# Moving half of a weight's column means to a later step, and two jobs from VectorE to ScalarE

## The chip, the cores and the metric

The kernel runs on one core of a Trainium2 chip. A core has a matrix engine (TensorE, "PE" in the profile), three engines for elementwise work (VectorE "DVE", ScalarE "ACT", GpSimd "POOL") and DMA queues. Each engine takes its own list of instructions in order and waits on semaphores for the others. TensorE writes into a small memory of accumulators, PSUM; VectorE and ScalarE read it[...]. The metric is the time of one execution in microseconds on the device, as the median of several runs.

## The reference: what is computed

Two blocks follow each other. The first is attention that keeps, for every query, only the 32 largest scores. The second mixes tokens and channels by a Fourier transform, normalises, and runs a two-layer network.

```python
# attention: q, k, v are (8 batches, 8 heads, 576 tokens, 64), float32
scores = (1 / sqrt(64)) * q @ k.transpose(0, 1, 3, 2)
kth = the 32nd largest of each row
scores = where(scores >= kth, scores, -1e9)
attn = exp(scores - rowmax); attn = attn / (attn.sum(-1) + 1e-9)
x = attn @ v                      # then (8, 576, 512): heads side by side

# Fourier mix and network: w_ch1 (512, 2048), w_ch2 (2048, 512)
mixed = real(fft(fft(x, axis=1), axis=2))
u = x + mixed
un = (u - mean(u)) / sqrt(var(u) + 1e-6)          # over the 512 channels
out = u + maximum(un @ w_ch1, 0) @ w_ch2
```

`(u - mean(u)) @ w1` equals `u @ (w1 - columnmean(w1))`. The kernel uses this: it takes each column's mean off `w1` once ("centring"), and then feeds the network with `u` that was never centred. The scale `1/sqrt(var)` is applied at the very end.

## The kernel before

The program is one long list of steps. A step handles one tile of attention rows: 9 tiles for each pair of heads, 4 pairs for each batch, so 36 steps for each of the 8 batches (`PER_BATCH = 36`). In step `i` VectorE finds the largest 32 scores of a tile (eight passes of `max` and `match_replace`), GpSimd and ScalarE mask and exponentiate an earlier tile, TensorE makes scores for a tile three steps ahead and transposes one that was exponentiated. Two functions place further work into steps: `at(step, where, fn)` appends `fn` to a slot of a step ("pe", "act", "dve", "pool" and others), and a queue of network units fills TensorE's remaining time.

The first 36 steps also load the weights. Each of 32 chunks is split by VectorE (line 162 and 165), converted by ScalarE (177, 179, 183, 184) and joined by GpSimd (192). Centring `w1` comes on top, 512 columns (`c`) at a time:

```python
    def centre(c):
        cols = slice(DM * c, DM * (c + 1))
        cm = ps_s.tile([P, DM], F32, name=f"cm_{c}", tag="sp")
        for dt in range(NDT):
            nc.tensor.matmul(
                cm, lhsT=ones, rhs=w1[:, dt, cols], start=(dt == 0), stop=(dt == NDT - 1)
            )
        mean = means[:, c, :] if c < 3 else sp1[:, 9 * WC:10 * WC]
        def subtract(dt):
            nc.gpsimd.tensor_tensor(
                out=w1[:, dt, cols], in0=w1[:, dt, cols], in1=mean, op=ALU.subtract
            )
        at(now[0] + 1, "convert", lambda: nc.scalar.copy(out=mean, in_=cm))
        for dt in range(NDT):
            at(now[0] + 1 + dt, "pool", lambda dt=dt: subtract(dt))
        return 3.5

    for c in range(DF // DM):
        at(start_of[n1] + 2 + 4 * c, "pe", lambda c=c: centre(c), 3.5)
```

`start_of[n1]` is 17, so the four products run at steps 19, 23, 27 and 31, and GpSimd has one subtraction in each of steps 20 to 35. The product `cm` lies in one of the two score buffers of PSUM (tag "sp") until ScalarE has copied it.

When the four pairs of a batch are done, its attention output is scaled by the softmax denominators and put into `x`, token rows by channels:

```python
        def normalise():                       # in to_tokens(pair, ch)
            nc.vector.tensor_tensor(           # line 479: two tiles of 128 rows
                out=x[:, 2 * ch:2 * ch + 2, cols]..., in0=tp[:, 0:2, :]..., in1=rd[:, 0:4]..., op=ALU.mult)
            if ch == 0:
                nc.vector.tensor_tensor(       # line 486: the tile of 64 tail rows
                    out=x[0:TAIL, 4, cols]..., in0=tp[0:TAIL, 2, :]..., in1=rd[0:TAIL, 4:6]..., op=ALU.mult)
        (late_now if at_once else late_next).append(normalise)
```

It runs twice for each pair of heads: for the even chunk (`ch == 0`, three tiles) and the odd one (two tiles). `rd` holds the inverse denominators, which VectorE makes (lines 457 and 460).

Then the tokens are folded (sums and differences of mirrored halves), so that the Fourier transform over tokens becomes two smaller products, one for the even half (`par == 0`) and one for the odd half:

```python
        def moved():                           # tail rows to the partitions of their mirror
            out, in_ = place(0)[0:TH, 2, :], x[TH:TAIL, 4, :]
            if eng[1] is nc.vector and eng[0] is nc.vector:
                nc.vector.tensor_copy(out=out, in_=in_)      # line 533
            else:
                nc.scalar.copy(out=out, in_=in_)             # line 535
...
        if first:                              # batch 0, T0 = 37
            def folds(b=b):
                for par, space in ((0, "own"), (1, "hT")):
                    for op in fold_steps(fold_ops(b, par, (nc.vector, nc.vector), space)):
                        op()
            at(T0, "dve", folds)
            ft, fc = (T0 + 1, T0 + 1), T0 + 1
```

For batch 0 VectorE does all folds at once in step 37; both token transforms (line 605), the channel transform (661), the row statistics and the first hidden units of the network (747) follow in steps 38 and 39. The last batch, too, folds its even half on VectorE alone. Hidden unit `it` reads columns `128*it` to `128*it + 127` of `w1`.

Of the kernel before, what the change touches and what calls it, by code (L numbers as in the profile page):

```python
# [9 lines left out]
F32 = mybir.dt.float32  # L10
# [8 lines left out]
P = 128  # L19
# [40 lines left out]
def kernel(  # L60
# [9 lines left out]
    nc = tc.nc  # L70
    B, H, S, D = q.shape
    DM = H * D
# [392 lines left out]
    def to_tokens(pair, ch, at_once=True):  # L465

        b, hp = divmod(pair, NPB)
        if b not in x_of:
            x_of[b] = batp.tile([P, 5, DM], F32, name=f"x_{b}", tag="x", bufs=2)
        x = x_of[b]  # L470
        xT, rd = xT_of.pop((pair, ch)), rd_of.pop((pair, ch))
        pool, tag = (ps_o, "o") if at_once else (ps_m, "mm")
        tp = pool.tile([P, 4, P], F32, name=f"tpx_{pair}_{ch}", tag=tag)
        for n, t in enumerate(CHUNKS[ch]):
            nc.tensor.transpose(tp[0:ROWS[t], n, :], xT[:, P * n:P * n + ROWS[t]], ident)  # L475
        cols = slice(P * hp, P * (hp + 1))

        def normalise():
            nc.vector.tensor_tensor(  # L479
                out=x[:, 2 * ch:2 * ch + 2, cols].rearrange("p t (e d) -> p t e d", e=2),  # L480
                in0=tp[:, 0:2, :].rearrange("p t (e d) -> p t e d", e=2),
                in1=rd[:, 0:4].rearrange("p (t e) -> p t e", e=2).to_broadcast([P, 2, 2, D]),
                op=ALU.mult,
            )
            if ch == 0:
                nc.vector.tensor_tensor(
                    out=x[0:TAIL, 4, cols].rearrange("p (e d) -> p e d", e=2),
                    in0=tp[0:TAIL, 2, :].rearrange("p (e d) -> p e d", e=2),
                    in1=rd[0:TAIL, 4:6].to_broadcast([TAIL, 2, D]),
                    op=ALU.mult,  # L490
                )

        (late_now if at_once else late_next).append(normalise)
        return 0.14 * len(CHUNKS[ch])


# [8 lines left out]
    def fold_ops(b, par, eng, space="own", mid=None):  # L505

        x = x_of[b]

        if space == "hT":
            sp = batp.tile([P, NIT * CW[0]], F32, name=f"fsp_{b}", tag="hT")

        def buf(n, name):
            if space == "hT":
                return sp[:, 3 * DM * n:3 * DM * (n + 1)].rearrange("p (s c) -> p s c", s=3)
            pool, tag = (batp, ("fold_s", "fold_d")) if space == "own" else (attp, ("PT0", "PT1"))
            return pool.tile([P, 3, DM], F32, name=f"{name}_{b}_{par}", tag=tag[n % 2], bufs=1)  # L520

        got = folded[b, par] = []

        def place(n):
            while len(got) <= n:
                got.append(buf(len(got), ("sd", "zw", "fg")[len(got)]))
            return got[n]

        def moved():

            out, in_ = place(0)[0:TH, 2, :], x[TH:TAIL, 4, :]
            if eng[1] is nc.vector and eng[0] is nc.vector:
                nc.vector.tensor_copy(out=out, in_=in_)
            else:
                nc.scalar.copy(out=out, in_=in_)

        def first(p):
            sd, op = place(0), ALU.add if par == 0 else ALU.subtract
            if p == 0:
                eng[0].tensor_tensor(out=sd[:, 0:2, :], in0=x[:, 0:2, :], in1=x[:, 2:4, :], op=op)  # L540
            else:
                s_ = sd[0:TH, 2, :]
                eng[1].tensor_tensor(out=s_, in0=x[0:TH, 4, :], in1=s_, op=op)

        def second(p):
            pp, ss = PARTS[p]
            s_, z_ = place(0)[pp, ss], place(1)[pp, ss]
            for cols, op in ((slice(0, Q2), ALU.add), (slice(Q2, DM), ALU.subtract)):
                (mid or eng[p]).tensor_tensor(
                    out=z_[:, :, cols], in0=s_[:, :, 0:Q2], in1=s_[:, :, Q2:DM], op=op  # L550
                )

        def third(n, p):
            pp, ss = PARTS[p]
            z_, f_ = place(1)[pp, ss], place(2)[pp, ss]

            def tt(out, up, down, op):
                eng[p].tensor_tensor(out=f_[:, :, out], in0=z_[:, :, up], in1=z_[:, :, down], op=op)

            if n == 0:  # L560
                eng[p].memset(f_[:, :, Q1:Q1 + 1], 0.0)
                eng[p].tensor_copy(out=f_[:, :, 0:DM:Q2], in_=z_[:, :, 0:DM:Q2])
                up, down = slice(1, Q1), slice(Q2 - 1, Q1, -1)
                tt(up, up, down, ALU.add)
                tt(slice(Q1 + 1, Q2), up, down, ALU.subtract)
            else:
                up, down = slice(Q2 + 1, Q3), slice(DM - 1, Q3, -1)
                tt(up, up, down, ALU.subtract)
                tt(slice(Q3, DM - 1), up, down, ALU.add)
                eng[p].tensor_copy(out=f_[:, :, DM - 1:DM], in_=z_[:, :, Q3:Q3 + 1])  # L570

        return {"moved": moved, "first": first, "second": second, "third": third}

    def fold_steps(f):

        def one():
            f["moved"]()
            f["first"](0)
            f["first"](1)

        def two():
            f["second"](0)
            f["second"](1)

        def three(n):
            f["third"](n, 0)
            f["third"](n, 1)

        return [one, two, lambda: three(0), lambda: three(1)]
# [287 lines left out]
    def at(step, where, fn, cost=0.0):  # L877
        plan.setdefault((step, where), []).append(fn)
        costs[step] = costs.get(step, 0.0) + cost
# [4 lines left out]
    WC = 512  # L884
# [18 lines left out]

    ones = batp.tile([P, P], F32, name="ones", tag="yt")
    nc.vector.memset(ones, 1.0 / DM)
    means = batp.tile([P, 3, DM], F32, name="means", tag="fold_d")

    def centre(c):
        cols = slice(DM * c, DM * (c + 1))
        cm = ps_s.tile([P, DM], F32, name=f"cm_{c}", tag="sp")  # L910
        for dt in range(NDT):
            nc.tensor.matmul(
                cm, lhsT=ones, rhs=w1[:, dt, cols], start=(dt == 0), stop=(dt == NDT - 1)
            )
        mean = means[:, c, :] if c < 3 else sp1[:, 9 * WC:10 * WC]

        def subtract(dt):
            nc.gpsimd.tensor_tensor(
                out=w1[:, dt, cols], in0=w1[:, dt, cols], in1=mean, op=ALU.subtract
            )  # L920

        at(now[0] + 1, "convert", lambda: nc.scalar.copy(out=mean, in_=cm))  # L922
        for dt in range(NDT):
            at(now[0] + 1 + dt, "pool", lambda dt=dt: subtract(dt))
        return 3.5

    for c in range(DF // DM):
        at(start_of[n1] + 2 + 4 * c, "pe", lambda c=c: centre(c), 3.5)

    for b in range(B):  # L930
        end = PER_BATCH * (b + 1) - 1
# [2 lines left out]
        T0 = end + (2 if first else 3 if soon else 4)  # L934
        if first:

            def folds(b=b):
                for par, space in ((0, "own"), (1, "hT")):
                    for op in fold_steps(fold_ops(b, par, (nc.vector, nc.vector), space)):
                        op()  # L940
            at(T0, "dve", folds)
            ft, fc = (T0 + 1, T0 + 1), T0 + 1
        elif soon:

# [233 lines left out]
```

## Time and profile before

| | |
|---|---|
| median time (3 runs) | 2011.47 us (2010.2 to 2012.25) |
| span of the profiled execution | 2010.3 us |
| TensorE busy | 1863.9 us, 93% |
| VectorE busy | 1641.2 us, 82% |
| ScalarE busy | 1220.3 us, 61% |
| GpSimd busy | 831.2 us, 41% |
| column-mean products (line 912) | 32 instructions, 18.3 us |
| subtractions (line 918) | 16 on GpSimd, 1.27 us each |
| normalisation on VectorE (line 479, line 486) | 64 of 424 ns, 32 of 273 ns |
| move of the tail rows on VectorE (line 533) | 3 of 415 ns |

An average over the span says little here, because the stages have different limits: the weights are loaded in roughly the first 260 us, batch 0 passes from attention to the network between 265 and 300 us, attention of later batches runs beside the network of earlier ones until 1800 us, and the last batch's network ends it. A line of the profile begins with the start in us and the duration; a bracket at its end tells how long the engine was idle before and which instruction ended the wait. A busy TensorE can still be waiting within a group, since ends of its pipelined instructions are modelled.

### The profile page before, as it was taken

The numbers are of one execution on the slowest core, as the hardware profiler recorded it, in microseconds if no ns is written. First come the engines' busy times: TensorE is split into PE (matmuls) and PEld (weight loads), VectorE is DVE, ScalarE is ACT, GpSimd is POOL, SyncE is SP. The second block draws the span as 40 slices with busy tenths as digits, with TensorE's granted clock in tenths as the row PEclk, the third lists the DMA queues.
The fourth block names the chain that finished last, engine by engine and source line by source line (L and its number), as shares of the span: only waits on it lengthen the run. The fifth ranks groups of instructions, "written<-read, shape, count | busy, mean of one in ns | idle before, by whom it ended". The sixth has DMA issues, their size and how long they took to land.

```text
span 2010.3 us, 27513 instructions
## 1 busy us (share of the span) xinstructions
PE 1863.9 (93%) x8626; PEld 1126.1 (56%) x8626; DVE 1641.2 (82%) x3405; ACT 1220.3 (61%) x3008; POOL 831.2 (41%) x1114
## 2 busy tenths in 40 slices
PE   5666679999889999999999999999999999998999
PEld 2333356465555656647565656647565656565655
DVE  7999889999999998988889888988899888853100
ACT  6878737677666766656665667656666667541100
POOL 4779822333433365234532374225533364223000
PEclk9678679999999999999999999999999999998999
DMA  4323100010000100001000001010000001000000
GB/s 128 96 82 100 54 7 19 24 26 24 23 19 24 27 24 24 18 18 26 24 24 13 26 19 29 18 32 18 19 24 24 23 15 30 0 14 1 11 14 11
DMA packets 133584, 57.81 MB, mean 29 GB/s; under 512 B 124352, under 2 KB 124480, under 8 KB 133440
## 3 DMA queue, kind: packets, MB, share of 16 engines
q1 hardware_dynamic: 132208, 55.73, 10.3%
q8 instruction: 69, 1.13, 0.2%
q14 instruction: 75, 0.61, 0.1%
q10 hardware_dynamic: 1232, 0.33, 0.1%
HBM read 46.57 MB, written 9.44 MB: 28 GB/s over the span
## 4 chain that ended last, share of the span: by engine, by line
PE 69%; DVE 12%; POOL 6%; ACT 6%; issue 6%; DMA 0%; SPq 0%; POOLq 0%; DVEq 0%
PE cp L771 20%; PE hp L747 20%; PE o L430 7%; PE sp L328 5%; PE tpP L393 5%; DVE m L349 5%; DVE wk L351 4%; PE yp L605 3%; POOL wk L366 3%; PE cp L807 2%; PE mp L661 2%; PE sp_t L298 1%; POOL w L192 1%; ACT wk L365 1%; ACT wk L372 1%
## 5 line engine op out<-in xcount | busy, mean ns | idle before, releaser
L366 POOL TENSOR_TENSOR wk<-S,wk 128x576 f32<-128x576 f32 x288 | 406.9, 1413 | 864.9 <-ACT wk L365 833.6
L349 DVE MAX8 m<-wk 128x8 f32<-128x576 f32 x864 | 623.1, 749 | 5.4
L747 PE MATMUL hp<-unT,w 128*128 128x256 f32 (+1 forms) x2048 | 538.3, 409 | 3.7 <-POOL t L709 2.2
L771 PE MATMUL cp<-w,hT 128*128 128x512 f32 x1024 | 479.3, 600 | 0.0
L747 PEld LDWEIGHTS hp<-unT,w 128*128 128x128 f32 x2048 | 372.7, 190 | 128.2 <-issue 32.2
L351 DVE MATCH_REPLACE8 wk<-m,wk 128x576 f32<-128x576 f32 x576 | 427.6, 742 | 0.0
L771 PEld LDWEIGHTS cp<-w,hT 128*128 128x128 f32 x1024 | 179.6, 190 | 183.6 <-issue 182.8
L372 ACT ACTIVATE wk<-wk,nt 128x576 f32<-128x576 f32 x288 | 225.0, 781 | 79.2 <-POOL wk L366 77.8
L365 ACT ACTIVATE wk<-S,nt 128x576 f32<-128x576 f32 x288 | 226.3, 786 | 50.0 <-POOL nt L358 47.8
L393 PE MATMUL tpP<-ident,wk 128*128 128x128 f32 x1152 | 186.8, 287 | 73.0 <-ACT wk L372 38.0
L396 ACT COPY PT<-tpP 128x512 f32<-128x512 f32 (+1 forms) x320 | 170.7, 544 | 117.4 <-PE tpP L393 114.9
L349 DVE MAX8 m<-S 128x8 f32<-128x576 f32 x288 | 214.1, 743 | 32.8 <-ACT S L302 32.5
L393 PEld LDWEIGHTS tpP<-ident,wk 128*128 128x128 f32 x1152 | 140.3, 146 | 174.2 <-ACT wk L372 56.7
L751 ACT ACTIVATE hT<-hp 128x320 f32<-128x320 f32 (+1 forms) x256 | 104.6, 409 | 192.2 <-PE hp L747 190.0
L351 DVE MATCH_REPLACE8 wk<-m,S 128x576 f32<-128x576 f32 x288 | 213.7, 742 | 0.0
L430 PE MATMUL o<-PT,v 128*64 128x256 f32 (+3 forms) x1440 | 195.9, 414 | 4.6 <-ACT PT L396 4.1
L331 ACT COPY S<-sp 128x512 f32<-128x512 f32 (+1 forms) x264 | 141.9, 588 | 73.3 <-PE sp L328 73.0
L328 PE MATMUL sp<-kT,qT 64*128 64x512 f32 (+1 forms) x528 | 168.1, 690 | 2.3 <-ACT means L922 1.9
L430 PEld LDWEIGHTS o<-PT,v 128*64 128x64 f32 x1440 | 111.5, 153 | 78.1 <-issue 14.6
L192 POOL TENSOR_TENSOR w<-w,space 128x512 f32<-128x512 f32 x96 | 123.6, 1287 | 8.6 <-ACT space L183 5.7
L785 DVE SCALAR_TENSOR_TENSOR x<-cp,gi,x 128x512 f32<-128x512 f32 x11 | 8.2, 746 | 128.3 <-PE cp L771 128.3
L479 DVE TENSOR_TENSOR x<-tpx,rd 128x256 f32<-128x256 f32 x64 | 27.1, 424 | 73.7 <-PE tpx L475 71.0
(125 smaller groups left out, 1899.0 us busy)
## 6 DMA issues: line engine op xcount, KB each, us to landing
space<-in_moe_w_ch_dram SPq DMA_DIRECT2D x32, 512.0 KB, 3.5
nat<-in_q_dram SPq DMA_DIRECT2D x128, 64.0 KB, 2.0
v<-in_v_dram SPq DMA_DIRECT2D x128, 64.0 KB, 2.1
out_dram<-x SPq DMA_DIRECT2D x32, 256.0 KB, 2.1
nat<-in_k_dram SPq DMA_DIRECT2D x124, 64.0 KB, 2.1
nat<-in_q_dram SPq DMA_DIRECT2D x128, 8.0 KB, 1.7
v<-in_v_dram SPq DMA_DIRECT2D x128, 8.0 KB, 1.7
nat<-in_k_dram SPq DMA_DIRECT2D x124, 8.0 KB, 1.7
```

What stands on the lines that cost most here:

```text
L192: nc.gpsimd.tensor_tensor(out=dst, in0=dst, in1=(low, high, ex)[part], op=ALU.mult if part else ALU.add,)
L328: nc.tensor.matmul(sp[r], lhsT=qT[hd, q_cols], rhs=kT[hd, :], start=True, stop=True)
L349: ops.append(lambda src=src, m8=m8: nc.vector.max(out=m8, in_=src))
L351: ops.append(lambda src=src, m8=m8: nc.vector.match_replace(w, m8, src, NEG))
L365: nc.scalar.activation(out=w, in_=Ssb[i], func=AF.Relu, scale=-FAR, bias=Nt[i][:, 1:2])
L366: nc.gpsimd.tensor_tensor(out=w, in0=Ssb.pop(i), in1=w, op=ALU.subtract)
L372: nc.scalar.activation(out=w, in_=w, func=AF.Exp, bias=Nt.pop(i)[:, 0:1], accum_out=den_t[pair % 3][:, c:c + 1],)
L393: nc.tensor.transpose(tp[:, c, :], p_sb[:, k0 + P * c:k0 + P * (c + 1)], ident)
L396: nc.scalar.copy(out=pt[:, NF * he:NF * (he + 1), col:col + w], in_=tp[:, :, o:o + w])
L430: nc.tensor.matmul(o[D * e:D * (e + 1), c0:c1], lhsT=vv[:, c, e, :], rhs=pt[:, 2 * NF if c == NF else NF * e + c, c0:c1], start=(c == 0), ...
L747: nc.tensor.matmul(hp[:, 0:w], lhsT=w1[:, dt, P * it:P * (it + 1)], rhs=unT[:, dt, 0:w], start=(dt == 0), stop=(dt == NDT - 1),)
L771: nc.tensor.matmul(cp, lhsT=hT[:, it, P * n:P * (n + 1)], rhs=w2[:, it, :], start=(it == 0), stop=(it == NIT - 1),)
```

## The change

It has four parts. The second half of the column means (`c` = 2 and 3) leaves the load stage: their products come at steps 36 and 37, their subtractions all at once in steps 39 and 40, before the network reaches these columns. The first half stays in the load stage, with the products at steps 19 and 27. This relieves GpSimd and TensorE while weights are being joined. The means of the second half get a tile of their own in the space of `x`. Next, the move of tail rows for folds done wholly by VectorE goes to ScalarE, ahead of the folds. Last, the normalisation of batch 1's output, all but its last piece, goes from VectorE to ScalarE, one step later, as single copies of 64 columns with a scale for each row. The aim is to take work off the engines that are full in each stage.

```diff
-        (late_now if at_once else late_next).append(normalise)
+        def normalise_on_act():
+            for n, t in enumerate(CHUNKS[ch]):
+                r = slice(0, ROWS[t])
+                for e in range(2):
+                    hd = slice(D * e, D * (e + 1))
+                    nc.scalar.mul(
+                        out=x[r, t, cols][:, hd], in_=tp[r, n, hd],
+                        mul=rd[r, 2 * n + e:2 * n + e + 1],
+                    )
+
+        if b == 1 and (hp, ch) != (NPB - 1, 1):
+            at(now[0] + 1, "act", normalise_on_act)
+        else:
+            (late_now if at_once else late_next).append(normalise)
@@ moved
-            if eng[1] is nc.vector and eng[0] is nc.vector:
-                nc.vector.tensor_copy(out=out, in_=in_)
-            else:
-                nc.scalar.copy(out=out, in_=in_)
+            nc.scalar.copy(out=out, in_=in_)
@@ fold_steps(f) becomes fold_steps(f, moved=True); with moved=False it leaves the move out
@@ centre
-    means = batp.tile([P, 3, DM], F32, name="means", tag="fold_d")
+    mean_of = {0: batp.tile([P, 2, DM], F32, name="means", tag="fold_d")}
-    def centre(c):
+    def centre(c, early):
...
-        mean = means[:, c, :] if c < 3 else sp1[:, 9 * WC:10 * WC]
+        if c == DF // DM // 2:
+            mean_of[1] = batp.tile([P, 2, DM], F32, name="means_1", tag="x", bufs=2)
+        mean = mean_of[2 * c // (DF // DM)][:, c % 2, :]
...
         for dt in range(NDT):
-            at(now[0] + 1 + dt, "pool", lambda dt=dt: subtract(dt))
+            s0 = now[0] + 1 + dt if early else now[0] + 3
+            at(s0, "pool", lambda dt=dt: subtract(dt))
...
     for c in range(DF // DM):
-        at(start_of[n1] + 2 + 4 * c, "pe", lambda c=c: centre(c), 3.5)
+        early = c < DF // DM // 2
+        at(
+            start_of[n1] + 2 + 8 * c if early else PER_BATCH - 2 + c, "pe",
+            lambda c=c, early=early: centre(c, early), 3.5,
+        )
@@ folds of batch 0
-            def folds(b=b):
+            def folds(b=b, T0=T0):
                 for par, space in ((0, "own"), (1, "hT")):
-                    for op in fold_steps(fold_ops(b, par, (nc.vector, nc.vector), space)):
-                        op()
-            at(T0, "dve", folds)
+                    f = fold_ops(b, par, (nc.vector,) * 2, space)
+                    at(T0, "act", f["moved"])
+                    for op in fold_steps(f, False):
+                        at(T0, "dve", op)
+            at(T0, "begin", folds)
```

More of the change, by code (lines that the diff above doesn't have):

```diff
@@ L572, in fold_ops, with fold_steps @@
         return {"moved": moved, "first": first, "second": second, "third": third}
-    def fold_steps(f):
+    def fold_steps(f, moved=True):
         def one():
-            f["moved"]()
+            if moved:
+                f["moved"]()
             f["first"](0)
```

## The prediction

> **What bounds the kernel now.** I first cut the span into stages by the busy time of each engine (columns: stretch in us; busy time of PE, weight loads, VectorE, ScalarE, GpSimd, with instruction counts; granted TensorE clock; DMA share; GB/s).
>
> ```profile
> 155.00:215.00 60.00, 37.85 (x184) 21.50 (x183) 56.79 (x116) 49.60 (x111) 58.38 (x55) 0.84 0.32 94
> 215.00:265.00 50.00, 31.38 (x134) 18.81 (x133) 38.97 (x80) 30.20 (x72) 35.57 (x34) 0.64 0.15 39
> 265.00:300.00 35.00, 28.94 (x135) 20.73 (x134) 31.30 (x77) 12.29 (x34) 5.61 (x12) 0.80 0.00 1
> 300.00:500.00 200.00, 198.87 (x946) 117.37 (x945) 193.84 (x398) 139.53 (x348) 66.26 (x88) 1.00 0.10 23
> 500.00:565.00 65.00, 57.01 (x299) 37.90 (x298) 64.09 (x139) 39.55 (x102) 30.53 (x46) 0.95 0.08 20
> 565.00:1800.00 1235.00, 1218.69 (x5819) 732.13 (x5818) 1084.65 (x2260) 804.32 (x2014) 509.99 (x738) 1.00 0.09 21
> ```
>
> From 565 to 1800 TensorE is idle for 16 us of 1235, so it sets the pace there, with the same work before and after the change. What is won earlier is therefore kept, and what matters is the stretch before 565. In 155 to 215 GpSimd is full (58.4 of 60). In 215 to 265 nobody is full, VectorE least expected of all: it lacks 11 us. From 300 to 565 VectorE has no gap except one of 2.8 us (258 of 265 us), and TensorE is full too until 500, then idles 8 us.
>
> Next, VectorE's own order of time in 226 to 266, with idle time and its releaser in brackets:
>
> ```profile
> 226.53 0.69 DVE L162 TENSOR_SCALAR wm<-space 128x512 int32<-128x512 int32 x1
> 231.16 0.69 DVE L165 TENSOR_SCALAR we<-space 128x512 int32<-128x512 int32 x1 [3.94 <-ACT w L177]
> ...
> 233.22 0.76 DVE L349 MAX8 m<-S 128x8 f32<-128x576 f32 x1 [0.71 <-ACT S L302]
> ...
> 244.58 0.30 DVE L457 TENSOR_SCALAR rd<-den 128x6 f32<-128x6 f32 x1 [1.88 <-ACT den L449]
> ...
> 248.53 0.76 DVE L349 MAX8 m<-S 128x8 f32<-128x576 f32 x1 [2.04 <-ACT S L302]
> ...
> 259.47 0.76 DVE L349 MAX8 m<-S 128x8 f32<-128x576 f32 x1 [0.67 <-ACT S L302]
> ...
> 265.15 0.42 DVE L479 TENSOR_TENSOR x<-tpx,rd 128x256 f32<-128x256 f32 x1 [1.00 <-PE tpx L475]
> ```
>
> And the chain of waits through the same time, for what stands behind the first gap:
>
> ```profile
> 222.99 5.75 PE cm L912 x8
> 228.74 0.45 PE tpP L393 x4
> 229.21 0.58 ACT PT L396
> 229.80 0.17 ACT PT L405
> 229.97 0.67 ACT wk L365
> 230.64 0.49 ACT w L177
> ```
>
> The reader is to see one cause. The last column-mean product (line 912) keeps TensorE for 5.75 us at the low clock; the transposes behind it come late, ScalarE waits for them with its copy (396), and the weight conversion (177) that VectorE's second split (165) needs stands behind that copy. Later on the same chain two subtractions of the last chunk of columns stand between joins and masks, at 250.0 and 253.7.
>
> [...] the granted clock is 0.50 in 220 to 225, 0.55 in 250 to 255 and 1.00 from 290 on, and the same eight instructions of line 912 took 3.67 us at 140.7 and 5.75 us at 223.0. [...] Here a 128x143 copy (638) takes 302 ns and the same with a scale operand (639) 414 ns, so 0.11 us.
>
> **The change, part by part.** (T is when the last normalisation before batch 0's folds starts, now 265.15.)
>
> 1. Steps 23 to 31. The second product goes from step 23 to 27, and its subtractions from 24–27 to 28–31. GpSimd's masks come every 6.62 us in steps with a subtraction (187.02 to 193.64: mask 1.4, three joins 3.9, subtraction 1.27), VectorE's splits every 6.14 us where it doesn't wait (187.59 to 193.73). So steps 24–27 become VectorE's. I add what VectorE idles: the interval 166.27 to 174.27 is 8.00 against 6.14, 1.86 too long, by the product at 165.96 (5.07 us); I take 1.5 of it. In 193.73 to 200.47 it loses 0.6, in 213.72 to 220.39 0.5, both with GpSimd behind; with the backlog cleared in 24–27 I take both. Sum: -2.6 us.
>
> 2. Steps 31 to 37. No product in step 31, no subtractions in 32–35. The gaps 3.94 and 0.71 go: -4.65. The later gaps 1.88, 2.04 and 0.67 (4.6 together) are ScalarE and TensorE catching up, with GpSimd's 4 x 1.27 in between; I take 3.3 of them. With part 1 this is -10.5 at T, 254.6. Were VectorE never idle, T would be about 252.
>
> Can TensorE follow, with the third product (c=2) in step 36? It stands after the q transposes (ending 256.6 now) and before the last tile's transposes (260.04 now, released by ScalarE; 3.4 us idle). At 3.7 to 5.8 us it takes the gap and 0.3 to 2.3 us more. At the new pace VectorE ends step 37 some 2 us after the tokens of the last tile could be there, so this about fits, and 0 is charged: the 1.3 us of gaps left in this part stand for it.
>
> 3. Step 37 and 38. The fourth product (c=3) comes after batch 1's 64-row scores (now 265.05) and before the tail scores. It waits until ScalarE has copied the first of these out of the two score buffers (about T+1.4), takes 5 to 5.8 us (T+7), and the next scores need its buffer back: mean copy to about T+8.9, two score products to T+10.5. So the token transform of the even half starts near T+10.5, now T+6.4 (271.54). It takes 6 us, and the odd half's 7.05 then start at T+16.5 instead of T+14.2 (279.33). Cost: +2.3 us.
>
> 4. The move of the tail rows. Two copies of 0.41 us (533) leave VectorE; a 32x512 copy on ScalarE takes 0.62 (535), where ScalarE has 23 of 35 us free. VectorE's odd fold is ready 0.9 us sooner, but by part 3 TensorE is late for it: 0. In the last batch one such copy (0.43 us at 1819.58) lies on the chain to a TensorE gap of 8.71 us that ends with the fold; there it counts: -0.4 us.
>
> 5. Subtractions at steps 39 and 40, 4 x 1.27 = 5.1 us each. The first four fall into GpSimd's free time between 303.9 and 311.0. The second four start about 312.6 and end at 317.7, and mask 40 (now 315.29) moves by 2.4 us, its exponential (now 317.88) by 1.2. TensorE's next transposes of that tile come at 323.5, so nearly nothing is lost: +0.3. The hidden layer's ninth block, the first that reads the late columns, runs at 328.
>
> 6. Batch 1's normalisation. Seven of eight go: on VectorE an even one costs 0.54 us from start to start (331.81 to 332.35), an odd one 0.34. 4 x 0.54 + 3 x 0.34 = 3.2 us, in a stretch where VectorE has no gaps until 563. ScalarE takes 6 or 4 instructions of 128x64 instead: a copy of that form 215 ns, with the scale operand some 0.3 us, so 1.8 and 1.2 us, 10.8 in all, against 60 us that it has free in 300 to 500. But TensorE is only 1.1 us short of full there, and gets idle time only after 500. I take three quarters: -2.4.
>
> Sum: -10.5 + 2.3 - 0.4 + 0.3 - 2.4 = -10.7 us. From 2011.5 this gives **2000.8 us**.
>
> **The rivals.**
> - *The products only change their place.* The two moved products run at low clock where the path is as narrow (the last tile's transposes, the folds' transforms), and what step 31 gives is taken back in 36 to 38. For it: the clock is 0.5 to 0.55 in half of the 5 us slices there, and 7.4 us each (3.7 at half clock) would cost about 2 us more at T and 2 at the transforms. Against it: TensorE idles 3.4 us before the tile's transposes and 4 of the 15 us from 265 to 280. It would give about -5: 2006.
> - *TensorE bounds batch 1.* It is full until 500, so the 3.2 us of VectorE only open gaps in VectorE, and the extra ScalarE work delays buffers for TensorE. For it: 198.9 of 200 busy. Against it: VectorE has no gap in all that time, and after 500 TensorE waits for it. Then part 6 is 0 or +1: 2003.
> - *The first stage gives more.* VectorE becomes gapless from 174 to T, and TensorE, now without a pause before the folds' transforms, gets its full clock there: the odd half at 280 to 286 runs at 0.50 and could fall from 7 to 5 us. Then -15 to -17: 1995.
>
> **Range and chances.** The largest term is part 2, 5 to 10 us by how many of the later gaps close; part 3 may be 0 to 4, part 6 0 to 3.2. Together the range that holds 8 in 10 is 1994 to 2006.5. A change of 2% would be 40 us; the gaps and subtractions concerned are not worth more than 17 us, and no added wait is near 40. Chances: faster by over 2% 0.01, within 2% 0.98, slower 0.01.
>
> **What would show it.** Part 1 and 2: no product between steps 27 and 36, the masks of steps 24–27 about 6.15 us apart, VectorE's five blocks of steps 33–37 each near 5.1 us, T near 254.6. Part 3: the odd half's transform starting 15 to 17 us after T; if it is 18 or more, the first rival holds. Part 5: mask 40 late, TensorE without a gap from hidden block to hidden block. Part 6: VectorE still gapless from step 41 to the statistics of batch 1, and these some 2.4 us closer to the start of batch 0's hidden layer; if VectorE shows gaps on ScalarE or TensorE instead, the second rival holds. I am wrong if the time is above 2006.5, most likely by the two moved products, or if a difference arises after 600.

## The result, and the profile after

| | before | after |
|---|---|---|
| median, in runs taken together | 2010.84 us (2009.45 to 2012.25, 6 runs) | 2004.12 us (2003.44 to 2004.36, 6 runs) |
| ratio | | 0.9966 [0.9953, 0.9979] |
| span of the profiled execution | 2010.3 us | 2002.2 us |

The change takes off 6.7 us where 10.7 had been predicted. (The same program measured again, further down, was only 0.8 us below before; where the difference lies is said there as far as it is known.) I first give the profile after, then a division of the span into stages that all experiments use.

The busy time of each engine by stretch, after (columns: stretch in us; length; busy time of PE, weight loads, VectorE, ScalarE, GpSimd, with instruction counts; granted TensorE clock; DMA share; GB/s):

```profile
155.00:215.00 60.00, 36.42 (x177) 21.73 (x177) 59.26 (x119) 49.96 (x112) 54.32 (x52) 0.76 0.32 94
215.00:265.00 50.00, 33.03 (x155) 18.54 (x153) 45.16 (x98) 34.24 (x81) 31.28 (x31) 0.75 0.15 40
265.00:300.00 35.00, 30.91 (x157) 23.80 (x159) 28.61 (x69) 11.10 (x30) 13.44 (x24) 0.90 0.00 0
300.00:500.00 200.00, 198.11 (x945) 115.78 (x942) 193.73 (x393) 144.67 (x383) 73.80 (x89) 1.00 0.10 25
500.00:565.00 65.00, 50.73 (x271) 33.45 (x269) 64.02 (x137) 41.11 (x107) 30.88 (x50) 0.94 0.10 23
565.00:1800.00 1235.00, 1224.57 (x5852) 737.75 (x5851) 1077.86 (x2247) 804.48 (x2011) 506.13 (x725) 1.00 0.09 21
```

In 155 to 215 the full engine has changed from GpSimd (58.4, now 54.3 of 60) to VectorE (56.8, now 59.3). In 215 to 265 VectorE lacks 5 us instead of 11. From 300 to 500 GpSimd and ScalarE have 7.5 and 5.1 us more to do, the late subtractions and the normalisation; the rest is nearly the same there.

VectorE in order of time through the end of the load stage, after (start, duration; a bracket is idle time and its releaser):

```profile
226.02 0.68 DVE L162 TENSOR_SCALAR wm<-space 128x512 int32<-128x512 int32 x1
226.61 0.68 DVE L165 TENSOR_SCALAR we<-space 128x512 int32<-128x512 int32 x1
...
237.98 0.27 DVE L457 TENSOR_SCALAR rd<-den 128x6 f32<-128x6 f32 x1 [0.64 <-ACT den L449]
...
241.93 0.76 DVE L349 MAX8 m<-S 128x8 f32<-128x576 f32 x1 [2.07 <-ACT S L302]
...
256.99 0.42 DVE L479 TENSOR_TENSOR x<-tpx,rd 128x256 f32<-128x256 f32 x1
```

The gap of 3.94 us between the two splits (162, 165) is gone. Of the three later gaps the one of 2.04 stays, the one of 1.88 shrinks to 0.64, the one of 0.67 is gone. T, the last line, is 256.99 instead of 265.15.

GpSimd's masks (366) on either side of step 31, first before, then after:

```profile
220.15 1.41 POOL L366 TENSOR_TENSOR wk<-S,wk 128x576 f32<-128x576 f32 x1
230.72 1.41 POOL L366 TENSOR_TENSOR wk<-S,wk 128x576 f32<-128x576 f32 x1 [3.94 <-ACT wk L365]
```

```profile
218.67 1.42 POOL L366 TENSOR_TENSOR wk<-S,wk 128x576 f32<-128x576 f32 x1
225.29 1.40 POOL L366 TENSOR_TENSOR wk<-S,wk 128x576 f32<-128x576 f32 x1
```

The interval falls from 10.57 to 6.62 us, the pace that GpSimd keeps in the steps around it. This one step is more than half of the whole gain.

And TensorE at batch 0's token transforms before:

```profile
271.54 3.89 PE L605 MATMUL yp<-fs,fg 128*128 128x145 f32 x16 [0.84 <-DVE fg L558]
...
279.33 7.05 PE L605 MATMUL yp<-fs,fsp 128*128 128x145 f32 x30 [1.81 <-DVE fsp L558]
```

and, from the late products on, after:

```profile
249.17 3.60 PE L924 MATMUL cm<-w,ones 128*128 128x512 f32 x8
...
257.91 3.70 PE L924 MATMUL cm<-w,ones 128*128 128x512 f32 x8 [0.89 <-ACT S L320]
...
264.90 2.25 PE L617 MATMUL yp<-fs,fg 128*128 128x145 f32 x16
...
271.15 7.15 PE L617 MATMUL yp<-fs,fsp 128*128 128x145 f32 x30 [1.91 <-DVE fsp L569]
```

Both late products (924) run at full speed (granted clock 1.00 from 248 to 270), 3.6 and 3.7 us, and the 16 instructions that open the even half's transform take 2.25 us, against 3.89 before (0.51 in 268 to 272, 0.63 in 272 to 276). But ahead of the odd half TensorE still pauses for VectorE's fold, 1.91 us where it was 1.81, its clock falls in this pause from 1.00 to 0.50 (at 270.4) as it did before (at 278.4), and the odd half takes 7.15 us, before 7.05.

**The stages.** The first column-mean product (c = 0, step 19; "product 0" below) is the same in every kernel here, and it starts anywhere from 137.97 to 141.09 us without any system. So I count from it. T is as in the prediction; "hidden" is batch 0's first hidden unit, "last" the first token transform of the last batch. All times in us, one profiled execution each.

| kernel | product 0 to T | T to hidden | hidden to last | last to end |
|---|---|---|---|---|
| before | 124.4 | 34.6 | 1531.5 | 179.1 |
| normalisation alone | 124.1 | 34.6 | 1531.3 | 179.2 |
| late subtractions alone | 124.1 | 37.8 | 1531.5 | 182.5 |
| batch 1's normalisation left out | 124.1 | 37.8 | 1531.5 | 182.5 |
| **after** | 117.2 | 34.7 | 1531.5 | 179.1 |
| after, repeated | 117.2 | 34.7 | 1531.4 | 182.5 |
| means alone | 117.2 | 34.7 | 1531.4 | 179.1 |
| without normalisation | 117.3 | 37.9 | 1531.6 | 179.1 |
| the same, repeated | 117.3 | 37.9 | 1531.6 | 179.2 |
| late half left out | 117.6 | 32.6 | 1533.1 | 179.1 |
| pause filled | 117.2 | 32.1 | 1534.2 | 179.0 |
| move a step early, without normalisation | 117.8 | 31.1 | 1531.4 | 179.1 |
| move a step early, with normalisation | 117.8 | 31.1 | 1533.0 | 181.6 |
| move two steps early, without normalisation | 117.1 | 31.1 | 1534.1 | 178.9 |

Two things are read from it. What the change does to the work is in the first column, 124.2 (the mean of the four above) to 117.2: -7.0 us. And most of what else differs fits the clock: columns two and four take values about 3.4 us apart.

### The profile page after: what moved, and what is told of

Read it like the earlier page. It is cut to its first block, busy times and chain, and to the rows that moved or that the text cites. A ratio compares the mean times of both kernels' runs of the same rounds, so it can differ in the third digit from the quotient of the medians.

```text
span 2002.2 us, 27534 instructions
## 1 busy us (share of the span) xinstructions
PE 1856.8 (93%) x8626; PEld 1122.8 (56%) x8626; DVE 1639.2 (82%) x3391; ACT 1230.1 (61%) x3047; POOL 835.0 (42%) x1114
## 3 DMA queue, kind: packets, MB, share of 16 engines
q1 hardware_dynamic: 132208, 55.73, 10.5%
## 4 chain that ended last, share of the span: by engine, by line
PE 70%; DVE 12%; issue 6%; ACT 6%; POOL 6%; DMA 0%; POOLq 0%; DVEq 0%; ACTq 0%
PE cp L783 20%; PE hp L759 19%; PE o L430 7%; PE sp L328 5%; PE tpP L393 5%; DVE m L349 5%; DVE wk L351 4%; PE yp L617 3%; POOL wk L366 2%; PE cp L819 2%; PE mp L673 2%; PE sp_t L298 2%; ACT wk L365 1%; ACT wk L372 1%; POOL w L192 1%
## 5 line engine op out<-in xcount | busy, mean ns | idle before, releaser
L298 PEld LDWEIGHTS sp_t<-kt,qT 128*128 128x128 f32 (+1 forms) x322 | 51.7, 188 | 62.6 <-issue 23.8
```

## The experiments

### The three parts, one at a time

*Means alone*: the change without the normalisation on ScalarE and without the move on ScalarE, so only the column means differ from the kernel before.

> Only the later half of the column means, as in the change; the tail rows are moved by VectorE and batch 1 is normalised by VectorE, as before. My theory (the whole gain is the load stage's, and the two late products cost nothing): the network of batch 0 starts about 8 us earlier than the 299.7 us of before, the time is 7 to 9 us below before, at least as good as the whole change. Rival (the normalisation carries a part of the gain, as I predicted with 2.4 us): 4 to 5 us below before.

*Normalisation alone*: the kernel before, with batch 1's normalisation on ScalarE.

> The kernel before with only batch 1's normalisation given to ScalarE. My theory (TensorE sets the pace of batch 1 until about 490 us, VectorE only gets gaps): VectorE is about 2.5 us ahead at 470 us and then waits for the token transposes and GpSimd's fold; the time is 0 to 1 us above before. Rival (VectorE sets the pace): 2 to 3 us below before.

*Without normalisation*: the change, with the one line of before in place of the added branch.

> The changed kernel with batch 1's normalisation back on VectorE. My theory: 0.5 to 1 us below the changed kernel, so 7 to 8 us below before. Rival (normalisation helps by 2.4 us): 4 to 5 us below before.

```diff
 means alone / without normalisation (both): against the change
-        if b == 1 and (hp, ch) != (NPB - 1, 1):
-            at(now[0] + 1, "act", normalise_on_act)
-        else:
-            (late_now if at_once else late_next).append(normalise)
+        (late_now if at_once else late_next).append(normalise)
```

| | median (range, runs) | ratio to before |
|---|---|---|
| means alone | 2004.11 us (2002.47 to 2006.55, 4) | 0.9956 [0.9941, 0.9971] |
| normalisation alone | 2010.62 us (2008.85 to 2016.6, 20) | 0.9996 [0.9989, 1.0003] |
| without normalisation | 2007.89 us (2006.57 to 2008.76, 9) | 0.9978 [0.9969, 0.9988] |

The means alone have the whole gain, the normalisation alone has none. The third run was a miss: 4 us slower than the means alone, although only the move of the tail rows separates them. Its trace is like that of the change up to 277 us and then differs in the clock. Here are stretches around it, of the change and then of the kernel without normalisation (columns as in the stage view above; the granted clock is third from the end):

```profile
266.00:270.00 4.00, 3.25 (x24) 2.30 (x22) 4.00 (x8) 1.48 (x7) 3.66 (x1) 1.00 0.00 0
270.50:277.00 6.50, 5.85 (x23) 4.37 (x23) 6.50 (x21) 0.00 (x0) 0.45 (x2) 0.50 0.00 0
277.50:284.00 6.50, 6.49 (x32) 4.72 (x31) 3.76 (x8) 2.04 (x7) 0.00 (x0) 1.00 0.01 3
```

```profile
266.00:270.00 4.00, 3.29 (x24) 2.35 (x22) 4.00 (x8) 1.48 (x6) 3.61 (x1) 1.00 0.00 0
270.50:277.00 6.50, 5.80 (x23) 4.33 (x23) 6.50 (x21) 0.00 (x0) 0.49 (x2) 0.50 0.00 0
277.50:284.00 6.50, 6.50 (x19) 5.30 (x18) 1.55 (x3) 2.15 (x7) 0.00 (x0) 0.50 0.01 3
284.50:290.00 5.50, 5.50 (x25) 3.95 (x25) 4.06 (x9) 0.00 (x0) 0.00 (x0) 1.00 0.00 0
```

In the first, half clock lasts until about 277.2, in the second until about 284.1, with TensorE busy for all of the extra time: 19 instructions where the other did 32. In slices of half a microsecond the two episodes (stretches of half clock) are 6.83 and 13.65 us long. In the change 8 instructions of line 617 take 2.27 us at a granted clock of 0.50 (at 1823.12) and 16 of the same form 2.25 us at 1.00 (at 264.90), so half of the time at half clock is lost. By an estimate from these numbers the longer episode costs 3.4 us more (half of 13.65 less 6.83), which is about the step between the values in the stage table (34.6, 37.9; 179.1, 182.5).

### Is it the products or the subtractions?

*Late subtractions alone*: the kernel before, all four products where they were, and only the subtractions of c = 2 and 3 moved to steps 39 and 40. It frees GpSimd of what the change frees it of, but not TensorE.

```diff
+        if c == DF // DM // 2:
+            mean_of[1] = batp.tile([P, 2, DM], F32, name="means_1", tag="x", bufs=2)
...
-            at(now[0] + 1 + dt, "pool", lambda dt=dt: subtract(dt))
+            s0 = now[0] + 1 + dt if early else PER_BATCH + 1 + c
+            at(s0, "pool", lambda dt=dt: subtract(dt))
```

> The kernel before with only the subtractions of the later half in steps 39 and 40; its two products stay in the load stage (steps 23 and 31). If the product of step 31 is the main cost there (my reading of the trace before: gaps of VectorE of 3.94 us and the ones after it), the last normalisation before the folds starts only 2 to 4 us earlier than the 265.15 us of before. If GpSimd's subtractions are the cost (rival), it starts 6 to 8 us earlier, as in the changed kernel (257.0 us).

Measured: 2010.62 us (2008.09 to 2017.39, 20 runs), ratio 1.0001 [0.9994, 1.0007]. Product 0 to T is 124.05 against 124.1 to 124.4: nothing, less than either theory had. The work that GpSimd loses is not what held the stage: with it gone, GpSimd only waits longer ahead of the mask of step 31, 5.78 us instead of 3.94.

```profile
228.67 1.40 POOL L366 TENSOR_TENSOR wk<-S,wk 128x576 f32<-128x576 f32 x1 [5.78 <-ACT wk L365]
```

What held the stage are the products in TensorE's order, step 31's above all. Whether the subtractions would cost anything once the product is gone is not shown, since no run moves the products alone. In the change GpSimd idles 0.89 to 3.68 us ahead of each of the four masks that follow the one at 225.29, and a subtraction takes 1.27.

*Late half left out*: the change without normalisation, and without the products and subtractions of c = 2 and 3 altogether (these columns stay uncentred).

```diff
-    for c in range(DF // DM):
+    for c in range(DF // DM // 2):
```

> The changed kernel without batch 1's normalisation on ScalarE, and with the later half of the column means left out altogether (products, copies, subtractions), so that half of w1 stays uncentred: the price of the late half. If the late products cost nothing because they fill pauses of TensorE and keep its clock at full speed, the normalisation before the folds starts at most 1 us earlier than 257.0 us, the even half's transform runs slower again (3 to 4 us for its first 16 instructions in place of 2.25), and from that normalisation to the first hidden unit it takes 34 us or more. If they cost what I predicted (2.3 us), it takes 32 to 33 us, and the time is 2 to 3 us below the changed kernel.

Measured: 2004.36 us (2002.29 to 2005.24, 8 runs), ratio 0.9966 [0.9955, 0.9976]. T does not come earlier (117.6 from product 0), so the product at step 36 costs nothing. The even half's first 16 instructions take 4.24 us instead of 2.25, about as long as in before (3.89), where the granted clock was 0.51 to 0.63 there; in the change it is 1.00, so by these times the late products keep TensorE's clock up. T to hidden was a miss, 32.6 where 34 or more was expected, and lies in the 32 to 33 us of the other side. But the late products do not delay the odd half: without them it starts later, at T+14.7 instead of T+14.2. It is shorter, 4.57 us instead of 7.15, because the slow even half ends later and leaves a pause of only 0.31 us ahead of it.

### The pause before the odd half

*Move a step early*: without normalisation, and ScalarE moves batch 0's tail rows at step 36, so that VectorE need not wait 1.43 us for this copy in the middle of its folds.

```diff
-                    at(T0, "act", f["moved"])
+                    at(T0 - 1, "act", f["moved"])
-            at(T0, "begin", folds)
+            at(T0 - 1, "begin", folds)
```

> As the previous one, and ScalarE moves batch 0's tail rows at step 36 instead of 37, ahead of batch 1's score copies. If VectorE's wait of 1.43 us for that move (seen in the changed kernel's trace at 260.1 us) is on the path, the folds end 1.4 us earlier; TensorE's pause before the odd half's transform falls from 1.9 to about 0.5 us, and if the low clock of that transform (7.15 us) comes from the pause it falls to about 4 us: together 3 to 5 us below the previous run. Rival (the pause does not matter for the clock, or TensorE is late anyway): 0 to 1.4 us below the previous run.

*Pause filled*: the change, with four products of 128x256 that nobody reads, put into TensorE's order between the two halves.

```diff
+                def fill():
+                    junk = ps_s.tile([P, DM], F32, name="junk", tag="sp")
+                    for _ in range(4):
+                        nc.tensor.matmul(
+                            junk[:, 0:DM // 2], lhsT=ident, rhs=fd[:, 0, :], start=True, stop=True
+                        )
...
+                at(ft[par], "pe1", fill)
```

> The changed kernel with four products of 128x256 that nobody reads, put into TensorE's pause of 1.9 us before the odd half's transform. If the pause costs the clock (granted 1.00 before it and 0.50 for 6 us after it), the odd half falls from 7.15 to 4 to 5 us and the time by 2 to 3 us, though TensorE does more. If the clock falls for another reason, the odd half stays at 7 to 8 us and the time rises by 0 to 0.5 us.

TensorE at the two transforms, first with the move a step early, then with the pause filled:

```profile
266.34 2.25 PE L603 MATMUL yp<-fs,fg 128*128 128x145 f32 x16
...
270.97 4.56 PE L603 MATMUL yp<-fs,fsp 128*128 128x145 f32 x30 [0.28 <-DVE fsp L555]
```

```profile
265.35 2.25 PE L617 MATMUL yp<-fs,fg 128*128 128x145 f32 x16
...
269.63 1.99 PE L1001 MATMUL junk<-fd,ident 128*128 128x256 f32 x8
271.61 4.56 PE L617 MATMUL yp<-fs,fsp 128*128 128x145 f32 x30
```

In both the odd half takes 4.56 us, against 7.15 in the change (all 30 instructions) and 8.08 without normalisation. So the pause is what drops the clock here: with junk in it, and nothing else changed, the episode is absent (granted clock 1.00 in all of 256 to 292), and T to hidden falls from 34.7 to 32.1. The times: the early move 2001.03 us (1999.62 to 2002.37, 4 runs), ratio 0.9939 [0.9922, 0.9955]; the filled pause 2004.51 us (2002.29 to 2004.71, 5 runs), ratio 0.9967 [0.9954, 0.998]. The first is 6.9 us below the run without normalisation, more than the 3 to 5 expected, because that run's half clock had lasted 13.7 us and not 6.8 as in the change; by the estimate above that costs 6.8 us, as much as T to hidden differs (37.9 and 31.1). For the second I had expected 2 to 3 us less than the change. What it won at 271 us it lost again by batch 3's first token transform (945 us): hidden to last is 2.7 us longer, about half of it lost before 727 us and half behind, where its trace has a new episode of 3.4 us near 790 (granted clock 0.79 in 788 to 796).

*Move two steps early*: as above, with `T0 - 2`.

> The change without the normalisation on ScalarE, and with batch 0's tail rows moved two steps early (at step 35). My theory: the move at step 36 delayed ScalarE's other copies and with them T by 0.8 us; at step 35 ScalarE has more room, so T comes back to about 257.0, TensorE has no pause of more than 1 us before the odd half's transform, the clock stays at full speed there (odd half 4.5 us rather than 7 to 8), and the time is 0 to 1.5 us below the 2001.0 of the move at step 36. Rival (any delay of ScalarE there costs the same): T stays near 257.8 and the time at 2001 or above.

Measured: 2004.02 us (2002.6 to 2005.84, 4 runs), ratio 0.9963 [0.9948, 0.9977]. Its mechanism came out (117.1 to T instead of 117.8, a pause of 0.93 us, no episode, odd half 4.56 us), its time did not: this profile too has an episode near 790 (0.90 in 784 to 788, 0.68 in 788 to 792), after a pause of 1.96 us, and hidden to last is 2.7 us longer, again about half of it ahead of that episode. The kernel with the move one step early has the same pause of 1.96 us there, and its clock stays at 1.00.

### The normalisation, and the change once more

*Normalisation left out*: the kernel before, with seven of batch 1's eight normalisations replaced by GpSimd writing zeros (batch 1's output is not computed). It shows what part 6 could bring at most.

```diff
+        def zeros():
+            nc.gpsimd.memset(x[:, 2 * ch:2 * ch + 2, cols], 0.0)
+            if ch == 0:
+                nc.gpsimd.memset(x[0:TAIL, 4, cols], 0.0)
...
-        (late_now if at_once else late_next).append(normalise)
+        if b == 1 and (hp, ch) != (NPB - 1, 1):
+            at(now[0], "pool", zeros)
+        else:
+            (late_now if at_once else late_next).append(normalise)
```

> The kernel before with seven of batch 1's eight normalisations left out; GpSimd writes zeros in their place, so ScalarE has no more work than before and the output of batch 1 is not the reference's. If TensorE sets the pace of batch 1 (my theory), the stretch from the first hidden unit of batch 0 to the end of batch 1's statistics stays at 263.0 us within 0.5. If VectorE sets it and ScalarE's added work ate the gain (rival), it is 2 to 3 us shorter.

Measured: 2010.94 us (2008.71 to 2017.43, 20 runs), ratio 1.0 [0.9993, 1.0007]; from the first hidden unit to the end of batch 1's statistics 263.29 us, before 263.02. Even with the work gone from both engines nothing is won. VectorE in the change (first), and with the means alone, where VectorE still normalises, shows why:

```profile
482.94 0.42 DVE L479 TENSOR_TENSOR x<-tpx,rd 128x256 f32<-128x256 f32 x1 [1.35 <-PE tpx L475]
...
491.92 3.16 DVE L560 TENSOR_TENSOR zw<-sd 128x512 f32<-128x512 f32 x4 [2.25 <-POOL sd L551]
```

```profile
485.80 0.42 DVE L479 TENSOR_TENSOR x<-tpx,rd 128x256 f32<-128x256 f32 x1
...
491.70 3.17 DVE L549 TENSOR_TENSOR zw<-sd 128x512 f32<-128x512 f32 x4
```

In the change VectorE does the last normalisation 2.9 us earlier, but only after waiting for TensorE's transposes (475), and then waits for GpSimd's fold (551). The fold behind both waits starts at 491.92 and 491.70, 352.1 and 351.7 us after product 0: the lead is all given back.

Three more runs were measured together with the move two steps early, on another chip than the experiments before it.

*The change again*, unaltered:

> The change as it is, on one chip with the next runs. My theory: how long the half clock lasts after the pause of 1.9 us before the odd half's transform is not settled by the program; so this can come out at 2004 with a half clock of 6 us, or at 2007 to 2008 with one of 14 us. Rival (the program settles it): 2004 and 6 us again, to a microsecond.

*Without normalisation, again*, unaltered:

> The change without the normalisation on ScalarE, for a second time. My theory: same code as the change up to that pause, so the 3.5 us between the two came from the length of the half clock and not from the normalisation; from batch 0's first hidden unit to the end of batch 1's statistics both take 263.3 to 263.8 us, and the two times overlap when measured side by side or differ by just what the half clock differs by. Rival (the normalisation on ScalarE is worth 3 us): this one is 3 us slower with a half clock of the same length.

*The change with the move a step early* (the early move above, with the normalisation on ScalarE):

> The whole change, normalisation on ScalarE included, with the move at step 36. With no pause before the odd half the clock has no part in it, so beside the run without the normalisation (2001.0) this tells part 6 alone. My theory (TensorE sets the pace in batch 1): 2000.5 to 2002. The prediction's part 6, or the rival that the normalisation is worth 3 us: 1998 to 1999.

| | median (range, runs) | ratio to before |
|---|---|---|
| the change again | 2010.55 us (2005.2 to 2011.94, 20) | 0.9992 [0.9985, 0.9999] |
| without normalisation, again | 2007.07 us (2002.3 to 2008.83, 13) | 0.9978 [0.997, 0.9987] |
| the change, move a step early | 2005.21 us (2003.68 to 2006.61, 6) | 0.9966 [0.9954, 0.9977] |

The change itself, 2004.12 us in its first six runs, is 2010.55 here, 0.8 us below before instead of 6.7; three of its 20 executions took 2005.2 to 2005.7 us, the others 2009.2 to 2011.9. Neither side of what I had written covers that. The profiled execution is one of the three: its load stage has the full gain (117.2), the half clock at 268.5 lasts 6.8 us again, and the 3.4 us that it has lost lie in the last batch. Granted clock there, third from the end, the change first, then its repeat:

```profile
1817.00:1824.00 7.00, 0.88 (x4) 0.91 (x5) 6.96 (x10) 0.00 (x0) 6.94 (x11) 0.72 0.00 0
1824.00:1831.00 7.00, 6.12 (x26) 4.33 (x26) 3.78 (x9) 0.04 (x1) 4.16 (x8) 0.55 0.00 0
1831.00:1838.00 7.00, 7.00 (x20) 3.27 (x19) 0.00 (x0) 1.70 (x6) 0.00 (x0) 1.00 0.00 0
```

```profile
1817.00:1824.00 7.00, 2.27 (x8) 1.95 (x8) 6.96 (x12) 0.00 (x0) 6.94 (x13) 0.50 0.00 0
1824.00:1831.00 7.00, 6.70 (x23) 4.82 (x24) 1.80 (x6) 1.50 (x6) 2.18 (x5) 0.50 0.00 0
1831.00:1838.00 7.00, 7.00 (x12) 2.83 (x11) 0.00 (x0) 0.33 (x2) 0.00 (x0) 0.70 0.00 0
```

At full load (7.00 of 7.00) the repeat does 12 instructions where the other does 20. Where the 17 longer executions lose another 5 us was not profiled; more such episodes would do it, but that is not shown.

On the normalisation these runs agree with the stage table. From the first hidden unit to the end of batch 1's statistics it takes 263.7 us with the normalisation on ScalarE and 263.4 without, as expected. Side by side, the kernel without it is now 3.5 us *faster* than with it, where in the first runs it had been 3.8 us slower. The two programs are the same both times, so the sign of this difference is not the code's; that the clock makes all of it is not shown, since most executions were not profiled. The early move with the normalisation is 2005.21, not the 2000.5 to 2002 of my theory, because 1.6 us more lie between hidden and last and 2.5 in the last batch. In the last batch half clock lasts 17 us, and 20 instructions there (line 783, at 1832.22) take 10.30 us; without the normalisation they take 8.85, as in the change, where half clock lasts 10 us. Most of the 1.6 us appears near 582, where VectorE waits 2.18 us for TensorE's transposes instead of 0.74; why is open. Its first two columns equal those of the early move without it, to 0.1 us.

## Why the prediction was right, and where it was wrong

The direction, the stage and the cause held in the first measurement: the time fell by less than 2%, inside the range, all of it before T, and through the removed product of step 31. In the second the gain before T was there again in the execution that was profiled, but the median of 2010.55 us lies above 2006.5, from where the prediction had called itself wrong, and only a part of that is traced to half clock. By its own steps:

1. **Part 1 (steps 23 to 31): -2.6 predicted, between -0.2 and +0.5 measured.** This step failed. From product 0 to VectorE's split at the end of this stretch (162 at 226.02, before at 226.53) it takes 86.20 us after, and 85.79, 86.40 and 86.38 in the three kernels with before's early products and subtractions. I had added up VectorE's gaps in the one trace of before. But in that trace VectorE stood 2.9 us further ahead at product 0 than in the other two (its split at 0.97 us ahead of the product, theirs 1.9 behind it), and its gaps only used up that lead. Nor did the longest of these gaps come from the product. The 1.86 us between 166.27 and 174.27 were laid to the product of step 23, but the change with the move a step early, which has no product there and VectorE with before's lead, shows the same gap (first before, then this kernel):

```profile
174.27 0.69 DVE L162 TENSOR_SCALAR wm<-space 128x512 int32<-128x512 int32 x1 [1.07 <-ACT w L177]
```

```profile
174.73 0.69 DVE L162 TENSOR_SCALAR wm<-space 128x512 int32<-128x512 int32 x1 [1.18 <-ACT w L177]
```

   The interval ahead of it is 8.16 us there, before 8.00, and 6.14 in the kernel with the normalisation alone, which has the product and no lead. With the same lead as before, this kernel and the repeat without normalisation reach the split after 86.25 and 86.24 us, 0.5 later than before. Without a lead, VectorE is full at once when GpSimd is relieved, as the 59.3 of 60 show.

2. **Part 2 (steps 31 to 37): -7.9 predicted, -6.8 measured** (from that split to T 37.8 us in the two such kernels beside before, 31.0 after; 38.6 in before, whose split comes 0.6 us sooner). The 4.65 us of the two first gaps went as predicted. Of the 3.3 us from the later gaps somewhat more than half came (1.88, 2.04 and 0.67 became 0.64, 2.07 and none); the gap of 2.07 at 241.93 stays. With part 1 the term of -10.5 should have been -7.0. That the third product would fit in step 36 at no cost held; of a share of the subtractions no run shows anything.

3. **Part 3 (products at steps 36 and 37): +2.3 predicted, 0 measured.** The fourth product came as described, and moved the even half from T+6.4 to T+7.9, not to T+10.5. I charged 5 to 5.8 us for it, as two of the early products took at low clock (5.07 and 5.75), and 6 for the even half. The clock was at 1.00 from 250 to 270, where before had 0.50 to 0.91 in the slices from 256 to 272, because the products themselves fill TensorE's pauses (with them left out, pairs of score products at 259 and 262 take 1.63 and 2.07 us, in the change 1.12): 3.7 us, and 2.25 for the first 16 instructions. The odd half began at T+14.16, before at T+14.18, and in both VectorE's fold released it, so TensorE had another 1.91 us to spare. I had the clock in the third rival only, and did not carry it into the sum.

4. **Part 4 (the move): 0 and -0.4 predicted, 0 measured.** With the means alone, where VectorE moves the rows, T to hidden is the same 34.7 us: in the change VectorE, spared the two copies of 0.41 us, waits 1.43 us for ScalarE's first copy. In the last batch the wait for the fold fell from 8.71 to 8.48 us, and hidden to last shows no difference.

5. **Part 5 (subtractions at steps 39 and 40): +0.3 predicted, 0 within 0.2 measured.** GpSimd and then TensorE in the change:

```profile
304.46 4.98 POOL L933 TENSOR_TENSOR w<-w,means 128x512 f32<-128x512 f32 x4
309.39 1.42 POOL L366 TENSOR_TENSOR wk<-S,wk 128x576 f32<-128x576 f32 x1
```

```profile
315.81 0.65 PE L393 MATMUL tpP<-ident,wk 128*128 128x128 f32 x4 [0.23 <-ACT wk L372]
```

   Mask 40 follows straight upon the four subtractions (4.98 us), and all that TensorE sees of it is 0.23 us.

6. **Part 6 (normalisation): -2.4 predicted, 0 measured.** The second rival was right: VectorE "without a gap" was only keeping step. That it is TensorE that sets the pace of batch 1 is read from its 198.9 busy us of 200 and from VectorE's wait for its transposes. From the first hidden unit to the end of batch 1's statistics the change takes 263.8 us, the means alone 263.4: nothing is won there either. The cost on ScalarE was right for one 128x64 piece, 331 ns where I had 0.3 us, but six in a row overlap and take 1.31 us (at 327.95), not 1.8. Against the 215 ns of a plain copy of this form (302) the scale operand adds 116 ns.

The first rival (products only change their place, 2006) falls: at their new place they cost nothing. The third was right on the clock up to 270 us and wrong at the odd half, where the pause of before, which this rival had thought gone, stayed and dropped it again (to 0.50); with the move a step early its 7 to 5 us is seen (7.15 to 4.56). The sum of what was measured is -7.0 + 0 + 0 + 0 + 0 = -7.0, against -6.7 in the times. That the total came no further off is in part luck: parts 1, 2 and 6 promised 5.9 us too much, part 3 charged 2.3 too much.

The fastest kernel here is the one with the tail rows moved a step early and without the normalisation on ScalarE, 2001.03 us; with that normalisation the same move gave 2005.21, no less than the change's first 2004.12. T to hidden is 31.1 us in all three kernels with an early move, 3.6 less than in the change, and their executions (four to six of each) spread over 2.8 to 3.2 us. With the late products and the pause left in, executions spread over 0.9 to 6.7 us and medians of the same program differ by up to 6.4. What decides between 6.8 and 13.7 us of half clock stays open. The kernel without normalisation had 13.7 both times and the change 6.8 both times, though both do the same work up to there; so do before and the kernel with batch 1's normalisation left out, and in these the odd half took 7.05 and 8.08 us, T to hidden 34.6 and 37.8. So the work ahead of the pause does not decide it alone.

## What to carry to other kernels

A gap on an engine is worth its length only if nothing else sets the pace: before adding gaps up, find out whether the engine was ahead at the start of the stretch, and count every stage from an event that all kernels share. Where TensorE pauses, ask what the pause does to the clock afterwards: useful work moved into it can be free, as the two late products were, and a pause of 1.9 us cost about 3.4 or 6.8 us more here, by the estimate from half clock of 6.83 and 13.65 us. When differences of a few microseconds are at stake, compare stages in the traces, since totals also carry what happens far from the edit, low-clock episodes among it.

## What the hardware showed that I had not expected

- A pause of 1.91 us was enough to halve the clock (1.00 to 0.50); it fell about 1.1 us into the pause. The pause of 1.81 us in before did the same, about 0.8 us into it. Pauses of 0.28 and 0.93 us at the same place did not do it (granted clock 1.00), and one of 1.96 us near 787 did it in one kernel (0.68 in 788 to 792) and not in another (1.00).
- At this place half clock ended only after 6.8 or 13.7 us, with nearly unbroken matmuls from about 0.8 us after its start. In the last batch episodes of about 10 us (the change), 14 (before), 17 (the change with the move a step early) and 20 (the change again) were seen. Short ones of 3.4 us occur too: near 503 us in the change, and near 510 and 524 in before, where the prediction had the clock at 1.00 from 290 on.
- One inverse-denominator instruction of VectorE (128x4, line 457) took 1.08 us at 205.85 while GpSimd ran a mask, and 0.29 us in the trace of before. Part of the slack that part 1 counted on went there.
